# Unread matmuls of zeros in seven other forms ahead of an attention and two-MLP kernel

## The chip, the cores and the metric

The kernel runs on one core of a Trainium2 chip. The metric is the device time of one launch in microseconds (us). A core has five engines that run side by side, each through an instruction list of its own, in order: TensorE (PE in the profile, its weight loads PEld), VectorE (DVE), ScalarE (ACT), GpSimd (POOL) and SyncE (SP), which here only issues DMAs. An engine waits for another by semaphores, which the tile framework sets from what each instruction reads and writes. TensorE's clock has two levels, 2.4 and 1.2 GHz; the profile gives the granted level as a share of the upper one (1.00 and 0.50).

## The reference, cut to what matters

Three parts, one after the other, in float32:

```python
# q, k, v [4, 8, 576, 64], f [4, 8, 576]
scores = q @ k.T / 8 + cum_i - cum_j        # cum = cumsum(log(clip(f))), causal
x = softmax(scores) @ v                     # -> [2304, 512]
h = x @ w_in                                # [512, 2048]
g = where(h >= 1, h, where(h <= -1, 0, (h + 1) ** 2 / 4))
x = g @ w_out                               # [2048, 512]
# the top two of 8 experts per token, softmax of their noisy logits as weights
out[t] += weight * (max(x[t] @ w1[e], 0) @ w2[e])   # w1 [512, 1024], w2 [1024, 512]
```

## The kernel before, in words

Most products are made with each operand split into a high and a low part of type float32r, three products for one. Attention works through 16 pairs of heads. For a pair, q and k come in by DMA, TensorE transposes them (`turn`, L377, and `turn_tail`, L381), ACT writes the high parts (`split_hi`, L397), DVE the low ones (`split_lo`, L401), a DMA swaps halves of k (`k2`, L421), POOL makes the differences of the cumulated decay (`diff`, L439, from `crow` and `ccol`, with a mask at L444), TensorE makes the scores (L468, L469; L457 for the last tile), DVE adds and takes the minimum (L482), ACT takes the exponential (L491), TensorE transposes it (L501), ACT and DVE split it into `aX` and `aY` (L524, L528), and TensorE multiplies with the values (L547). The cumulated sums themselves come from DVE's clip (L290), ACT's logarithm (L292) and DVE's scan (L293); for the first pair TensorE spreads the rows (L343) and turns them into columns (L300), which DVE copies into `ccol` (L304). The first MLP's units (L682, L708) and the conversion of its weights (L644 to L652) are mixed in between; routing and the experts come after.

The order of every engine's list up to the experts is worked out when the kernel is built: `job` registers a piece of work for an engine with its inputs, outputs and an estimated cost, `in_order` plays a model of the engines and returns the jobs in one order, and `emit` writes them out. Engines then keep to their lists. Ahead of the jobs only a few constants are made (L74 to L84), among them `ident`, the identity.

In `emit`, ahead of a job of TensorE that the model says comes after a gap, products `ident` x `ident` are written into the bank `idle` (L217); nobody reads them. The first of these stand ahead of the transposes of the first k. Each such float32 product appears in the trace as two instructions.

`zeros` (L313) is a set of POOL jobs: memsets of `qt`, `vnat`, `e4`, then `aX[0]`, `aX[1]`, `aY[0]`, `aY[1]`. In POOL's list small memsets and iotas (L357, L739 to L747) follow, and then the first `diff`.

PSUM's banks are rings: `psS` (tag "s", two banks, scores), `psT` (two, transposes), `psA` ("av", one), `psH` ("h", one, which `idle` holds at first) and `psY` (two; the first pairs' transposes of q and k are in it).

Of the kernel before, what the change touches and what calls it, by code (L numbers as in the profile page):

```python
# [8 lines left out]
F32 = mybir.dt.float32  # L9
# [7 lines left out]
BIG = 1.0e9  # L17
# [5 lines left out]
def kernel(  # L23
# [56 lines left out]
    # rows 2 r and 2 r + 1 of a product, summed  # L80
# [14 lines left out]
    class Ring:  # L95
        """Buffers that take turns."""
# [8 lines left out]
    class Buf:  # L105
        """One use of a ring's buffer; the tile is there when the first job that names it is emitted."""
# [8 lines left out]
    class Job:  # L115
        """Instructions of one engine that are emitted together."""
# [7 lines left out]
    def job(eng, cost, at, fn, r=(), w=(), size=0):  # L124
        """r, w: what the job reads and writes: buffers, (buffer, part), or names."""
        j = Job(len(jobs), eng, cost, fn, at, size)
        jobs.append(j)
        for x in r:
            if x in writer:
                j.deps.add(writer[x])  # L130
            readers.setdefault(x, []).append(j)
        for x in w:
            if x in writer:
                j.deps.add(writer[x])
            j.deps.update(readers.get(x, ()))
            writer[x], readers[x] = j, []
        j.deps.discard(j)
        for x in (*r, *w):
            b = x[0] if isinstance(x, tuple) else x
            if isinstance(b, Buf) and b not in j.bufs:  # L140
                if not b.jobs:
                    j.new.append(b)
                b.jobs.append(j)
                b.left += 1
                j.bufs.append(b)
        return j

    def in_order():
        """The jobs in the order in which engines that take whatever is due first would start them."""
# [7 lines left out]
        for j in jobs:  # L157
            # a bank isn't taken before all that its users wait for is on its way
            held = {d for b in j.new if b.held for u in b.jobs for d in u.deps if d.no < j.no}
            for d in (held | {b.jobs[0] for b in j.bufs}) - j.deps - {j}:  # L160
                d.after.append(j)
                j.left += 1
# [4 lines left out]
        while len(out) < len(jobs):  # L167
            best = None
            for e, todo in ready.items():
                pick = None  # L170
                for j in todo:
                    t = max(j.ready, free[e])
                    for i, b in enumerate(j.new):
                        # buffers of the same ring come one after the other
                        k = len(b.ring.tenants) + sum(o.ring is b.ring for o in j.new[:i])
                        if b.ring.fixed and b.no != k:
                            t = 1e9
                        k -= b.ring.bufs
                        if k >= 0:
                            o = b.ring.tenants[k]  # L180
                            t = max(t, o.free) if not o.left else 1e9
                    if t < 1e9 and (pick is None or (t, j.at, j.no) < pick[:3]):
                        pick = t, j.at, j.no, j
                if pick and (best is None or pick[:3] < best[:3]):
                    best = pick
# [20 lines left out]

    def emit():
        # TensorE's clock halves after a stretch of little work: until the first MLP takes the bank,
        # products that nobody reads keep each stretch busy enough
        idle, last, busy = psH.tile([P, 512], F32, name="idle", tag="h"), WARM2, []  # L210
        for j in in_order():
# [61 lines left out]
    # Y: head 0's last TAIL queries, the queries before them of the head at hand, head 1's last TAIL queries  # L273
    aY = [ap1.tile([P, NKB, YQ // TAIL + 1, TAIL], F32R, name=f"aY{i}") for i in range(2)]
    e4 = ap1.tile([P, NKB * P], F32, name="e4")
    # the last query tile holds both heads' last TAIL rows; each head's stationary operand is zero in the other's columns
# [45 lines left out]
    class Pair:  # L322
        """Two heads; their queries go through in tiles of P rows, the last tile holds the last TAIL rows of both."""
# [7 lines left out]
        def add(self):  # L331
# [7 lines left out]
            for j in range(2 * (self.n == 0)):  # L339
                # the first rows by way of the tensor engine  # L340
# [24 lines left out]
        def prep(self):  # L365
            """Transposed q' = -q / 8 and k in (hi, lo) parts.

            t = q'.k + cum_j - cum_i has the row's maximum as its minimum, negated."""
# [14 lines left out]
            # head 0: [hi; lo], head 1: [lo; hi] on the partitions  # L383
# [19 lines left out]
            for i, w in enumerate((1, 0, 2)):  # L403
# [7 lines left out]
                for j in range(2):  # L411
                    # parts of qk: queries, keys, the last keys
# [12 lines left out]
        def tile(self, n, j, it):  # L425
            """Decay differences and scores; softmax's exponentials; transposed, in (hi, lo) parts."""
# [5 lines left out]
            # cum_j - cum_i, with BIG where j is behind i  # L432
# [100 lines left out]
        def values(self, n, j, x):  # L533
            """Attention times values, transposed: the sum of the two halves of the partitions."""
# [3 lines left out]
            for kb in range(nkb):  # L538
                # the first column that isn't all zero; head 0's last queries come first
# [22 lines left out]
        def finish(self):  # L562
            """1 / (sum + 1e-9), by head and tile, as rows; the second head's last rows are its last tile's first."""
# [32 lines left out]
    class Quarter:  # L596
        """QF hidden units' weights in a slot."""
# [29 lines left out]
    def convert_quarter(q, at, pace):  # L627
        """A quarter's float64 weights, given as int64 bits, as exact pairs of float32r; also kept in DRAM.

        The high word as a float32, times 2**-112, has float64's exponent less 896 in its bits:  # L630
        float32's, with the fields three bits too low. Magnitudes under 2**-119 come out tiny."""
# [23 lines left out]
    def load_x(at, c, x, eng):  # L655
        """A chunk of the attention's output, transposed, in (hi, lo) parts."""
# [9 lines left out]
    class Unit:  # L666
        """Two blocks of hidden units of one chunk: up, the nonlinearity, down into the chunk's sums."""
# [4 lines left out]
        def up(self, at, j):  # L672
# [16 lines left out]
            # max(h, 1) * ((clip(h, -1, 1) + 1) / 2) ** 2  # L689
# [34 lines left out]
    def routing_consts():  # L724
        for i, src in enumerate((moe2_w_gate, moe2_w_noise)):
            dma(30, lambda i=i, src=src: nc.sync.dma_start(wg[:, :, i * E:(i + 1) * E], src.rearrange("(c p) e -> p c e", p=P)), [("xd", 0, 0)], [("wg", i)], size=16384 * 8)
        # no key of the last block is visible to the queries before the last tile
# [32 lines left out]
    class Route:  # L760
        """Top two experts of some tiles of tokens, their weights and places in the experts' lists."""
# [7 lines left out]
        def turn(self, at, t, xt, dep):  # L769
            """One tile's rows, transposed, and its logits."""  # L770
# [20 lines left out]
        def chain(self, at):  # L791
# [20 lines left out]
            # log1p(exp(z)) = log(u) * e / (u - 1), u = 1 + e; e where u = 1  # L812
# [31 lines left out]
            # the largest two, the first of equals first  # L844
# [18 lines left out]
            # places in the experts' lists: the tile's rows before, and the tile's totals  # L863
# [23 lines left out]
            # the place r goes to partition r % P, unit r / P  # L887
            @part("DVE", 0.36 * K, ["ecol"], ["base"])
            def _():
# [4 lines left out]
                if self.seal:  # L894
                    # the first two experts' first EARLY places are for the tokens up to here; what stays empty is a pad
                    ts(base[:, 0, :2], base[:, 0, :2], float(EARLY), None, op0=OP.max)
# [102 lines left out]
    def stream(at, rate, units, end=True):  # L999
        """Pieces of units; a unit's down after the next one's up, in the next call's if this isn't the end."""  # L1000
# [53 lines left out]
    def expert_jobs(e, rings, stages, at, pace, deps=()):  # L1054
        """An expert's w1 [DM, F2] and w2 [F2, DM] as (hi, lo) with the contraction on partitions."""
# [69 lines left out]
    def counts():  # L1125
        """How many blocks each expert has."""
# [6 lines left out]
        # the second expert's second block of CH is always done  # L1133
        nc.vector.scalar_tensor_tensor(odd[:, 1:2], units[:, 1:2], 4.0, odd[:, 1:2], op0=OP.is_gt, op1=OP.mult)
        # 2: the odd block has P / 2 rows at most
# [11 lines left out]
    def early_block(at, e, r):  # L1147
        """The first EARLY places of one of the first two experts, while the rest is on its way."""
# [98 lines left out]
    # work by step; within a step by key  # L1247
# [16 lines left out]
    def bank_tr():  # L1264
        """A bank for transposes."""
# [3 lines left out]
    def expert(e, pool, lands):  # L1269
        """w1 [DM, F2] and w2 [F2, DM] as (hi, lo) with the contraction on partitions, and the work in pieces."""  # L1270
# [28 lines left out]
    def fetch(n, dst, g, cols, wait):  # L1299
        """Rows of the list's tokens, transposed, in (hi, lo) parts."""  # L1300
# [16 lines left out]
    def when(n, i, cols):  # L1317
        """The first of two tiles of rows is through before the last piece of work."""
# [17 lines left out]
    def blend(n, cols, ys):  # L1336
        """Rows of the result as they are, plus the weighted rows of an expert."""
# [6 lines left out]
    def combine(n, py, cols, quick=False):  # L1344
        """Rows of the result plus an expert's weighted rows."""
# [16 lines left out]
    def body256(x, W, cols, side=None, quick=False):  # L1362
# [19 lines left out]
        def down(fp, k):  # L1382
            hh, hl = (h.rearrange("p (j t) -> p j t", j=2) for h in hs[fp % 2])
            # of the last two blocks of hidden units, one tile of rows after the other
# [65 lines left out]
    def body64(x, W, idc, g):  # L1450
        """P / 2 rows: (hi, lo) side by side, so that the products with the weights' hi part take one pass."""
# [48 lines left out]
    def last_units():  # L1500
        """The last unit's column of each list."""
# [33 lines left out]
    for e in range(E):  # L1535
        nblk, nodd = size[2 * e:2 * e + 2]

        # the block that is always done here
# [77 lines left out]
```

## Time and profile before

| | |
|---|---|
| Median of 3 runs | 1269.96 us (1266.02 to 1273.33) |
| Span of the profiled execution, first to last instruction | 1250.6 us |
| The median less that span | 19.4 us |
| PE busy | 1166.6 us, 93% |
| DVE, POOL, ACT busy | 65%, 47%, 41% |
| Mean granted clock of TensorE | 0.981 |

The profile was taken of one execution; the time of that execution as a launch is not listed beside the three, so the median stands for it: what lies around the span is then 19.4 us. A row of the timeline is: start us, duration us, engine, line, operation, output and inputs, count, and in brackets how long the engine was idle before and who released it; neighbouring instructions of one line are merged into one row. A matmul's duration contains its way through the array; how often one can follow the other is read from the distance of starts.

### The profile page before, as it was taken

Reading aid. Unit: us, or ns where it says so; the run is one execution under the profiler, and the core shown is the slowest. Engines: PE = TensorE matmul, PEld = TensorE weight load, DVE = VectorE, ACT = ScalarE, POOL = GpSimd, SP = SyncE. Lnnn points to the kernel's source line nnn. Section 1 sums busy time; section 2 is a strip of 40 time slices with the busy share of each in tenths; the row PEclk is TensorE's granted clock in tenths of the full one; section 3 lists DMA queues with packets and bytes.
Section 4 is the critical chain, followed back from the end, with each engine's and each line's share of the span. In section 5 each row is a group of like instructions: output and inputs, shape, how many; then the busy total and the mean of one; then the engine's idle time right before and its main releaser. Section 6 shows DMA issues by size and latency. Waiting matters only on the chain. (4 is left out here: it accounts for less than half of the span.)

```text
span 1250.6 us, 21814 instructions
## 1 busy us (share of the span) xinstructions
PE 1166.6 (93%) x7527; PEld 1040.7 (83%) x7527; DVE 813.6 (65%) x1814; ACT 517.5 (41%) x1151; POOL 587.8 (47%) x724
## 2 busy tenths in 40 slices
PE   8787799999999999999999999999999999899994
PEld 6676688889888988998999998888888888788893
DVE  7989889986876657734565685373555555774432
ACT  6767776667654664623344351120312121330000
POOL 7779777767474654620300114353434343434221
PEclk8989999999999999999999999999999999999997
DMA  6777798855745434664022143262434343642121
GB/s 169 205 221 202 235 312 247 272 167 153 219 158 150 119 111 134 191 259 162 16 78 67 43 128 122 71 212 91 158 113 155 119 163 107 218 156 70 54 73 38
DMA packets 135314, 185.56 MB, mean 148 GB/s; under 512 B 72063, under 2 KB 81569, under 8 KB 135157
## 3 DMA queue, kind: packets, MB, share of 16 engines
q1 hardware_dynamic: 122692, 148.85, 38.3%
q0 software_dynamic: 12464, 34.76, 8.5%
q8 instruction: 81, 1.33, 0.4%
q14 instruction: 77, 0.62, 0.2%
HBM read 134.76 MB, written 41.65 MB: 141 GB/s over the span
## 5 line engine op out<-in xcount | busy, mean ns | idle before, releaser
L682 PEld LDWEIGHTS h<-xc,w 128*128 128x128 f32 x1344 | 170.8, 191 | 10.2 <-issue 5.4
L682 PE MATMUL h<-xc,w 128*128 128x256 f32 x1344 | 173.6, 285 | 4.2 <-DVE ga L696 4.1
L439 POOL TENSOR_TENSOR D<-crow,ccol 128x128 f32<-128x128 f32 (+4 forms) x160 | 136.4, 859 | 60.5 <-DVE mn L482 51.8
L708 PE MATMUL y<-w,gh 128*128 128x512 f32 x480 | 156.6, 407 | 0.0
L1379 DVE TENSOR_SCALAR hs<-eh 128x512 fp32r<-128x512 f32 x64 | 44.0, 688 | 131.9 <-PE eh L1375 131.9
L921 POOL DMA_INDIRECT lists<-ent,ai x36 | 36.7, 1019 | 147.4 <-DVE ai L912 122.3
L1262 POOL TENSOR_TENSOR ys<-ys,prev 128x512 f32<-128x512 f32 x32 | 41.8, 1306 | 132.6 <-ACT ys L1324 123.0
L708 PEld LDWEIGHTS y<-w,gh 128*128 128x128 f32 x480 | 84.9, 191 | 14.5
L708 PE MATMUL y<-w,gl 128*128 128x512 f32 x240 | 95.5, 398 | 0.0
L699 POOL TENSOR_TENSOR gl<-ga,gh 128x512 fp32r<-128x512 f32 x48 | 62.5, 1302 | 66.3 <-ACT gh L697 61.1
L695 ACT ACTIVATE ga<-ga,half 128x512 f32<-128x512 f32 x72 | 52.1, 723 | 97.7 <-DVE ga L694 78.5
L1262 ACT CAST e<-w 128x512 fp32r<-128x512 f32 x96 | 56.2, 620 | 76.9 <-DMA w<-in_moe_w_dram 72.5
L1375 PE MATMUL eh<-xF,e 128*128 128x256 f32 x672 | 84.8, 282 | 3.1 <-PEq L1581 3.1
L1389 PE MATMUL y<-e,hs 128*128 128x512 f32 x336 | 85.5, 400 | 1.0 <-DVE hs L1379 1.0
L694 DVE TENSOR_SCALAR ga<-h 128x512 f32<-128x512 f32 x60 | 41.4, 689 | 69.0 <-PE h L682 63.5
L1375 PEld LDWEIGHTS eh<-xF,e 128*128 128x128 f32 x672 | 82.2, 189 | 4.7 <-issue 3.5
L491 ACT ACTIVATE et<-et,mn 128x128 f32<-128x128 f32 (+3 forms) x128 | 72.0, 564 | 16.7 <-DVE mn L482 15.7
L482 DVE CUSTOM_DVE_ANT_0 et<-s,D 128x128 f32<-128x128 f32 (+3 forms) x128 | 61.2, 484 | 23.9 <-PE tr L501 12.3
L1262 DVE TENSOR_TENSOR e<-w,e 128x512 fp32r<-128x512 f32 x96 | 72.8, 795 | 5.7 <-ACT e L1262 5.7
L1389 PEld LDWEIGHTS y<-e,hs 128*128 128x128 f32 x336 | 60.5, 188 | 13.9 <-issue 1.4
L1332 POOL DMA_INDIRECT out_dram<-ys,ids x32 | 33.7, 1053 | 77.2 <-DVE ys L1262 38.4
L1144 POOL DMA_INDIRECT xg<-x2d,ids x48 | 50.5, 1052 | 29.4 <-issue 22.3
(307 smaller groups left out, 2794.6 us busy)
## 6 DMA issues: line engine op xcount, KB each, us to landing
w<-in_moe_w_dram SPq DMA_DIRECT2D x128, 256.0 KB
w<-wsd SPq DMA_DIRECT2D x24, 1024.0 KB
wsd<-w SPq DMA_DIRECT2D x16, 1024.0 KB
crow<-cumd SPq DMA_DIRECT2D x30, 288.0 KB
k<-qk SPq DMA_DIRECT2D x60, 144.0 KB
st<-in_moe_w_in_dram SPq DMA_DIRECT2D x16, 512.0 KB
st<-in_moe_w_out_dram SPq DMA_DIRECT2D x16, 512.0 KB
D<-rsd SPq DMA_DIRECT2D x32, 144.0 KB
```

The lines of the kernel that those rows point to most:

```text
L439: nc.gpsimd.tensor_tensor(Dt.t[r, :w], self.crow[i].t[r, :w], ccol[r, it, h:h + 1].to_broadcast([r.stop - r.start, w]), op=OP.subtract)
L482: nc.vector.tensor_tensor_reduce(out=ev()[:, c0:c0 + pw], in0=ps.t[:, :pw], in1=Dt.t[:, c0:c0 + pw], scale=1.0, scalar=HUGE, op0=OP.add, o ...
L491: nc.scalar.activation(ev()[:, :w], ev()[:, :w], AF.Exp, bias=mn.t[:, 0:1], scale=-1.0, accum_out=self.sm.t[:, j, it:it + 1])
L682: nc.tensor.matmul(h.t[:, j, :], self.quarter.up(2 * self.fp + j, db, wi), x[:, xi, db, :], start=(i == 0), stop=(i == 3 * NB - 1))
L695: job("ACT", 0.62, at - 2.4, lambda: nc.scalar.activation(a.t, a.t, AF.Square, bias=half, scale=0.5), w=[a])
L699: lambda: e.tensor_tensor(gl.t, a.t, r32(gh.t), op=OP.subtract), [a, gh], [gl])
L708: nc.tensor.matmul(self.py[t].t, g[:, j, ts], self.quarter.down(f, wi), start=(self.first and j == 0 and i == 0), stop=(self.last and j == ...
L1144: nc.gpsimd.indirect_dma_start(out=xg[gi], out_offset=None, in_=x2d[:rows, :], in_offset=bass.IndirectOffsetOnAxis(ap=idc, axis=0), **skip)
L1262: fn(*args)
L1375: nc.tensor.matmul(p[:, j, :], wt[:, db, fs], x[:, xi, db, :], start=(i == 0), stop=(i == 3 * NB - 1))
L1379: nc.vector.tensor_scalar(hh, ph[fp % 2], 0.0, None, op0=OP.max)
L1389: nc.tensor.matmul(py[t], h[:, j, ts], wt[:, fb, :], start=(fb == 0 and i == 0), stop=(fb == NF - 1 and i == 2))
```

## The change

Ahead of the first job, `emit` calls a new function `probes`. It takes the bank that `idle` holds, one use of `psA`'s bank and one of `psS`'s, has VectorE fill `aX[0]` with zeros, and issues 65 matmuls of these zeros and 4 transposes of `ident` on TensorE. Nobody reads what they write. With the float32r tile as operands (`z`) there are 16 of 512 columns, 5 each of 128, 256 and 512, 8 of 512 columns over half the rows (upper and lower half in turn), and 4 of 512 that alternate with the transposes. With the same bytes as float32 (`zf`) there are 3 of 256 columns, 3 over the upper half of the rows, 8 over upper and lower half in turn, and 8 that fill the left and right half of the output's partitions in turn. All else in the diff is comments and docstrings.

```diff
+    def probes(bank):
+        b2 = psA.tile([P, 512], F32, name="probe2", tag="av")
+        b3 = psS.tile([P, 512], F32, name="probe3", tag="s")
+        z = aX[0].rearrange("p i c -> p (i c)")
+        zf = r32(z)
+        nc.vector.memset(zf, 0.0)
+        mm = nc.tensor.matmul
+        for _ in range(16):
+            mm(bank, z[:, :P], z, start=True, stop=True)
+        for n in (128, 256, 512):
+            for _ in range(5):
+                mm(b2[:, :n], z[:, :P], z[:, :n], start=True, stop=True)
+        for _ in range(3):
+            mm(bank[:, :256], zf[:, :P], zf[:, :256], start=True, stop=True)
+        for _ in range(3):
+            mm(b2[:, :256], zf[:64, :P], zf[:64, :256], start=True, stop=True)
+        for _ in range(4):
+            mm(bank[:, :256], zf[:64, :P], zf[:64, :256], start=True, stop=True)
+            mm(b3[:, :256], zf[64:, :P], zf[64:, :256], start=True, stop=True)
+        for _ in range(4):
+            mm(b2[:64, :256], zf[:, :64], zf[:, :256], start=True, stop=True)
+            mm(b2[64:, :256], zf[:, 64:P], zf[:, :256], start=True, stop=True)
+        for _ in range(4):
+            mm(bank, z[:64, :P], z[:64], start=True, stop=True)
+            mm(b3, z[64:, :P], z[64:], start=True, stop=True)
+        for _ in range(4):
+            mm(b2, z[:, :P], z, start=True, stop=True)
+            nc.tensor.transpose(bank[:, :P], ident, ident)
+
     def emit():
         idle, last, busy = psH.tile([P, 512], F32, name="idle", tag="h"), WARM2, []
+        probes(idle)
         for j in in_order():
```

## Rows read from the trace of the kernel before

**Rows 1.** Timeline of TensorE (PE) from the start to the first scores.

```profile
1.47 4.16 PE L217 MATMUL idle<-ident 128*128 128x128 f32 x22 [1.47 <-DVE ident L76]
5.47 0.60 PE L377 MATMUL y<-ident,kn 128*128 128x128 f32 x4
...
8.92 1.12 PE L343 MATMUL s<-xf,ident 32*128 32x512 f32 x2 [2.51 <-DVE xf L293]
9.88 0.37 PE L300 MATMUL tr<-ident,xf 32*128 32x32 f32 x4
...
13.42 1.22 PE L217 MATMUL idle<-ident 128*128 128x128 f32 x4
14.30 0.56 PE L468 MATMUL s<-qk 128*128 128x256 f32 x1
...
18.24 0.61 PE L217 MATMUL idle<-ident 128*128 128x128 f32 x4
```

**Rows 2.** Timeline of VectorE (DVE), the same stretch.

```profile
1.77 0.06 DVE L84 MEMSET half<- 128x1 f32 x1
...
1.89 0.54 DVE L291 MEMSET k<- 32x576 f32 x1
...
8.90 0.68 DVE L401 SCALAR_TENSOR_TENSOR qk<-y,qk 64x512 fp32r<-64x512 f32 x1
...
11.36 0.32 DVE L304 COPY ccol<-tr 128x160 f32<-128x160 f32 x1
...
17.14 0.56 DVE L482 CUSTOM_DVE_ANT_0 et<-s,D 128x384 f32<-128x384 f32 x1 [1.06 <-PE s L469]
...
18.21 0.69 DVE L482 CUSTOM_DVE_ANT_0 et<-s,D 128x512 f32<-128x512 f32 x1 [0.50 <-PE tr L501]
```

**Rows 3.** Timeline of GpSimd (POOL) and ScalarE (ACT), the same stretch.

```profile
1.77 0.99 POOL L313 MEMSET aX<- 128x512 f32 x2
...
6.50 0.34 POOL L747 IOTA e<- 128x8 int32 x1
...
7.39 1.19 ACT L397 ACTIVATE qk<-y 64x512 fp32r<-64x512 f32 x2
...
11.84 0.97 POOL L439 TENSOR_TENSOR D<-crow,ccol 128x128 f32<-128x128 f32 x2 [5.00 <-DVE ccol L304]
```

**Rows 4.** Stretches: bounds, length, each engine's busy us (count), granted clock, DMA share, GB/s.

```profile
9.90:11.90 2.00, 1.91 (x13) 1.34 (x12) 1.88 (x8) 1.82 (x4) 0.06 (x1) 0.86 0.47 107
...
14.20:17.20 3.00, 3.00 (x14) 2.92 (x13) 0.79 (x5) 2.11 (x5) 2.84 (x5) 0.50 0.52 117
17.20:18.30 1.10, 1.10 (x6) 0.88 (x5) 0.60 (x3) 0.15 (x1) 1.02 (x2) 0.55 0.78 157
...
93.00:125.00 32.00, 24.09 (x165) 19.98 (x163) 30.13 (x83) 25.26 (x71) 28.88 (x41) 1.00 0.71 199
```

**Rows 5.** TensorE's timeline at 700 us, products of 512 columns.

```profile
699.71 0.40 PE L708 MATMUL y<-w,gh 128*128 128x512 f32 x1
699.95 0.40 PE L708 MATMUL y<-w,gl 128*128 128x512 f32 x1
700.18 2.97 PE L682 MATMUL av<-xc,w 128*128 128x256 f32 x24
```

**Rows 6.** The chain that ended last, one piece: start, us, what.

```profile
1162.82 5.62 PE eh L1375 x48
```

**Rows 7.** Line L217: count, shortest/median/longest ns, first and last start.

```profile
L217 PE MATMUL idle<-ident x186: 271/275/582, 1.5 to 135.5; 128*128 128x128 f32 x186
```

**Rows 8.** Waits, first 300 us (us in total, times, longest): SyncE's queue.

```profile
SPq L644 <- POOL w L652: 35.1, 14, 7.0
...
SPq L317 <- PE av L381: 13.5, 5, 7.0
SPq L317 <- PE y L381: 6.6, 3, 3.3
```

**Rows 9.** Waits of TensorE, first 300 us.

```profile
PE s L468 <- DVE mn L482: 8.7, 9, 3.2
```

## The prediction

> **What bounds the kernel now.** I read TensorE's timeline from the start first, because the change stands ahead of everything else in that list. It has three things to see [rows 1]: the unread products from 1.47 us, the transposes of the first k at 5.47, and the first scores at 14.30. Then the same stretch on the engines that feed the scores. DVE begins the low parts of k at 8.90 and copies `ccol` at 11.36 [rows 2]; POOL has been through its memsets and iotas by 6.84 (6.50 + 0.34), sits idle for 5.00 us until `ccol` is there, and starts the first difference at 11.84 [rows 3]. So the head is one chain through all engines: k's transposes, ACT's and DVE's splits, `ccol`, POOL's differences, DVE's minimum. Last I read who waits for whom in the first 300 us. SP, which issues all loads, waits 35.1 us for POOL to be through with the buffers of converted weights, and 13.5 and 6.6 us for TensorE's transposes to free the buffers of k and q [rows 8]; TensorE waits longest for DVE's minimum, 8.7 us [rows 9]. In a stretch of 32 us there TensorE is busy for 24.09 and DVE for 30.13 [rows 4]. No queue in this stage runs free of the engines: what starts late stays late.
>
> **What is added on TensorE.** Unread products do run: 186 of them stand in the trace of before [rows 7]. I price the new ones by distance between starts.
> - float32r, 512 columns: three starts lie 0.47 us apart over two [rows 5], 0.235 each. There are 16 + 5 + 4 = 25 over the whole height: 5.88 us. The 8 over half the rows would be 1.88 at the same distance.
> - float32r, 256 columns: 48 in 5.62 us [rows 6], 0.117 each; five are 0.59. At 128 columns no float32r product is in the trace. Half of 0.117 and the 0.235 of 512 columns are the ends (0.29 and 1.18 for five); I take 0.117, the nearest row, 0.59.
> - float32, 256 columns: not in the trace either. `idle`'s are float32 with 128 columns, two instructions per product. Four of them at 18.24 us took 0.61 to the end of the last [rows 1]; less its own 0.27 [rows 7] that is 0.34 over three starts, 0.113. Twice the columns and two instructions make 0.45 a product. L343 checks it from the other side: 512 columns, two instructions, from 8.92 to 9.88 [rows 1], so 0.48 for half. There are 3 + 3 + 8 + 8 = 22: 9.9 us.
> - Four transposes: four of k's took 0.60 to the end of the last [rows 1], less 0.27 and over three starts 0.11 each: 0.44.
>
> Together 5.88 + 1.88 + 0.59 + 0.59 + 9.9 + 0.44 = 19.3 us if each waits for the one before. To this comes a slow beginning. The first 22 `idle` instructions took 4.00 us (1.47 to 5.47) where 22 x 0.113 would be 2.5 [rows 1]. The other group of four, at 13.42, needed 0.88 to the next start, 0.22 each [rows 1], in a stretch around the granted clock 0.50, which is 1.2 GHz [rows 4]. So the list begins at the lower level, and what I pay for that is the 1.5 us that the 22 paid. 20.8 us.
>
> The unsettled price is that of the halves. No pair of half-height or half-width products on different halves is in the trace. L343, with 32 rows, is no faster for its small height: 0.48 per instruction of 512 columns, as the check above says. By this nearest row each of the 24 products (8 float32 by rows, 8 by columns, 8 float32r by rows) costs what a whole one does, 3.6 + 3.6 + 1.88 us, which is in the sum. The other end is that the two of a pair run at once: half of that, 4.54 us less. I take the row, and keep the other as a rival. The Trainium skill ("TensorE: Matmul & The Clock Gate", Part 3: Packing small matmuls) says that products in different row groups or column groups of the array overlap; its "TensorEngine Tiling (Array Packing)" (Key Properties) says that a change of the tiling mode drains the engine. By the first the sum is 16.3 us, and by the second each of five changes adds about 0.16 (0.27 less 0.11), 0.8 us by estimate; no row here shows either.
>
> **Where it lies.** The zeros come first: `half` ends on DVE at 1.83, and 32 x 576 zeros took 0.54 [rows 2], so 512 columns about 0.48. The probes begin near 2.4 and end at 23.2. The 22 `idle` instructions stand behind them, now at the upper level: 2.5 us. k's transposes start at 25.7 instead of 5.47, 20.2 late.
>
> Not all of that goes on, since what used to come late is waiting by then. DVE's first low part follows after 0.6 of transposes, half of ACT's 1.19 [rows 3] and 0.1, at 27.0; before it was at 8.90, held back by the scan. It is 18.1 late. POOL has a wait of its own: its memset of `aX[0]` overwrites what the probes read, so the whole list behind it stands until 23.2. From 1.77 to 6.84 POOL needed 5.07 us [rows 3], so it is free at 28.3. `ccol` ended 2.78 after DVE's first low part (11.68 less 8.90 [rows 2]), so now at 29.8, behind that: POOL's memsets hide, with 1.5 us to spare, and the first difference at 29.9 is 18.1 late as well. If the probes ended without freeing `aX[0]`, POOL would cost up to that much more. The loads behind POOL, ACT and TensorE on SP shift alike [rows 8]. VectorE's extra memset costs nothing: DVE waits for f and later for TensorE anyway.
>
> A part comes back. From about 11.3 to 18.2 us the granted clock was 0.50 (worked out from the 0.86, 0.50 and 0.55 of three stretches [rows 4]), not long after TensorE had stood idle for 2.51 us [rows 1]. DVE waited 1.06 and 0.50 for TensorE in it [rows 2]. After 23 us of work and with all inputs at hand the clock should be full there: 1.56 back (none, if it falls again). 18.1 - 1.6 = 16.5 us. Nothing later changes: the lists are the same.
>
> The profiled span, 1250.6, becomes 1267.1. With the 19.4 us by which the median lies above that span, 1286.5; I say 1286.
>
> **The rivals.**
> - The pairs run at once. 4.5 us less on TensorE, which leaves 12.0: 1282. For it: the two of a pair write different banks or partitions. Against: only L343's price, which is of single products.
> - The clock falls during the probes. In the trace it fell to 0.50 soon after the 32-row products of L343, behind an idle stretch, and came back only near 18.2, though TensorE was busy for 3.00 of 3.00 us [rows 4]. If products of half the height don't hold it either, a stretch like that one (6.9 us at the lower level) costs 3.4 us, and the 1.6 at the first scores doesn't come back: 1286.5 + 5.0 = 1291.5.
> - The delay is taken back, and the kernel isn't slower. One mechanism: TensorE's gaps in the first 150 us (about 8 us in 32 [rows 4]) would have to be gaps before loads that SP issues when it likes; two such stretches would swallow the 16 us, and 1270 would stay. It decides from the point where SP's weight loads are issued as early as before. Against: these gaps end with DVE, and SP waits for POOL and TensorE [rows 8, 9]. To be faster, it would also need fewer stretches at 0.50 later on, and one such stretch is worth 3.4 us.
> - The change doesn't do what it says: the probes are dropped, and 1270 stays. The 186 unread products that ran speak against it.
>
> **How the numbers follow.** Forecast 0.47, pairs at once 0.32, clock 0.14, taken back 0.05, dropped 0.02. Each case has some 3.5 us to either side from the spread of the runs before (1266.02 to 1273.33). The low end is the pairs' 1282 less 3.5 and a little, 1278; the high end the clock's 1291.5 with 1.5 us of dearer 128-column and float32 products, 1293. The forecast's own range is 1282 to 1290. About 0.5%, 6.35 us, can be told from no change: slower means over 1276.3. The three cases that are slower hold 0.93, the other two mostly fall within, 0.05, and 0.02 stays for faster.
>
> **What would show it.** In the changed trace: the first probe near 2.4 us; starts 0.235 apart at 512 columns; the half-height and half-width stretches at 3.6, 3.6 and 1.9 us, or at half of these; k's transposes near 25.7; POOL's memset of `aX` just before; the first difference near 30; the first scores' stretch at clock 1.00; from there every landmark the same 16 us late to the last instruction. The prediction is wrong if the delay at 30 us and that at 280 us differ by more than 4 us, or if the probes take under 16 or over 24 us.

## The result: slower, by less than forecast, and the profile after

The changed kernel takes 1279.27 us (median of 10 runs, 1271.66 to 1283.84) against 1266.9 for the kernel before (10 runs, 1262.59 to 1273.33). The ratio is 1.0086 [1.0062, 1.011]: 10.9 us more, 7.9 to 13.9. It was timed a second time later (e10 below): 1.0115 [1.0082, 1.0148], 14.6 us. The forecast was 16. Of the 6.7 us between the 1286 named and the 1279.27 measured, 3.1 are the median of before, which came out lower with more runs; the other 3.7 are the forecast's own (12.4 us between the medians against 16; by the ratio it is 5 too many).

TensorE's timeline from the start, in the changed kernel; "..." stands for rows of the same forms:

```profile
2.43 5.26 PE L216 MATMUL idle<-aX 128*128 128x512 f32 x16 [2.43 <-DVE aX L213]
7.53 2.47 PE L219 MATMUL probe<-aX 128*128 128x128 f32 x15
9.84 1.46 PE L221 MATMUL idle<-aX 128*128 128x256 f32 x6
11.22 1.34 PE L223 MATMUL probe<-aX 64*128 64x256 f32 x5
12.20 0.48 PE L226 MATMUL probe<-aX 64*128 64x256 f32 x1
12.40 0.38 PE L223 MATMUL probe<-aX 64*128 64x256 f32 x1
12.52 0.38 PE L226 MATMUL probe<-aX 64*128 64x256 f32 x1
12.62 0.38 PE L225 MATMUL idle<-aX 64*128 64x256 f32 x1
12.73 0.38 PE L226 MATMUL probe<-aX 64*128 64x256 f32 x1
...
14.44 0.43 PE L228 MATMUL probe<-aX 128*64 128x256 f32 x1
...
14.92 0.38 PE L228 MATMUL probe<-aX 128*64 128x256 f32 x1
14.93 0.38 PE L229 MATMUL probe<-aX 128*64 128x256 f32 x1
...
16.01 0.38 PE L229 MATMUL probe<-aX 128*64 128x256 f32 x1
16.32 0.49 PE L231 MATMUL idle<-aX 64*128 64x512 f32 x1
...
17.44 0.50 PE L234 MATMUL probe<-aX 128*128 128x512 f32 x1
...
18.92 2.62 PE L248 MATMUL idle<-ident 128*128 128x128 f32 x22
21.37 0.60 PE L408 MATMUL y<-ident,kn 128*128 128x128 f32 x4
...
28.61 0.56 PE L499 MATMUL s<-qk 128*128 128x256 f32 x1
```

The probes take from 2.43 to 18.92, 16.5 us and not 20.8. The whole-height forms cost what was worked out: 5.10 us to the next form for the first 16, 2.31 for the mixed 15 (1.18 + 0.59 + 0.59 forecast), 1.38 for the three float32 ones. The halves did not: their price was set too high. At 14.92 and 14.93 a left and a right half start together; the upper and lower halves of the float32 rows start 0.11 apart where one alone needs 0.21. From the first pair (12.20, 14.44, 16.32) to the next form the three stretches are 2.24, 1.88 and 1.12 us against 3.6, 3.6 and 1.88.

GpSimd (POOL) and VectorE (DVE) in the same stretch, which answer to [rows 2, 3]:

```profile
19.03 0.99 POOL L344 MEMSET aX<- 128x512 f32 x2 [17.19 <-PE probe L234]
23.25 0.68 DVE L432 SCALAR_TENSOR_TENSOR qk<-y,qk 64x512 fp32r<-64x512 f32 x1 [17.87 <-ACT qk L428]
26.19 0.97 POOL L470 TENSOR_TENSOR D<-crow,ccol 128x128 f32<-128x128 f32 x2 [2.29 <-DVE ccol L335]
...
31.45 0.56 DVE L513 CUSTOM_DVE_ANT_0 et<-s,D 128x384 f32<-128x384 f32 x1 [1.06 <-PE s L500]
32.52 0.69 DVE L513 CUSTOM_DVE_ANT_0 et<-s,D 128x512 f32<-128x512 f32 x1 [0.50 <-PE tr L532]
```

k's transposes are 15.9 us late, DVE's first low part 14.35, the first difference 14.35, the first scores 14.3. GpSimd is held by the probes for 17.19 us and then still waits 2.29 for `ccol`. The waits of 1.06 and 0.50 that I let go are there as before. Some stretches (bounds, length, busy us of PE, PEld, DVE, ACT, POOL with counts, granted clock, DMA share, GB/s; one row left out) show why:

```profile
21.40:22.20 0.80, 0.80 (x9) 0.56 (x7) 0.00 (x0) 0.19 (x1) 0.80 (x2) 1.00 0.00 0
...
23.50:25.50 2.00, 0.99 (x8) 0.78 (x7) 1.88 (x7) 1.72 (x6) 0.40 (x4) 1.00 0.60 150
25.50:27.70 2.20, 2.20 (x6) 1.02 (x4) 1.53 (x8) 1.49 (x4) 1.51 (x5) 0.56 0.43 96
27.70:30.00 2.30, 2.30 (x11) 2.27 (x11) 0.94 (x4) 1.93 (x4) 2.23 (x5) 0.50 0.56 128
```

TensorE comes out of the probes at 1.00, is busy for 0.99 of 2.00 us around the 32-row products, and by the first scores it is at 0.50, 1.2 GHz, as it was without probes [rows 4].

The profile's span is 1282.0 us, 31.4 more than before's. That is no measure of the change: the 1282.0 belong to a run of 1283.84 us, so only 1.8 us lie around a span, and the execution profiled before, 1250.6, was shorter than any of the 10 timed beside it (the shortest, 1262.59, would have a span near 1260.8). What differs is the second half. First and last starts of the experts' first block, in this order, with the span: before 1250.6, changed 1282.0, and of the experiments below e6 (no probes) 1264.1, e9 (probes four times) 1314.0, e2 1269.8 and e11 1279.7 (one and the same program):

```profile
L1193 PE MATMUL h<-xF,w x96: 274/281/365, 723.2 to 760.9; 128*128 128x256 f32 x96
```
```profile
L1224 PE MATMUL h<-xF,w x96: 274/281/365, 739.9 to 778.7; 128*128 128x256 f32 x96
```
```profile
L1202 PE MATMUL h<-xF,w x96: 274/281/365, 723.4 to 761.5; 128*128 128x256 f32 x96
```
```profile
L1225 PE MATMUL h<-xF,w x96: 274/281/365, 780.8 to 818.5; 128*128 128x256 f32 x96
```
```profile
L1224 PE MATMUL h<-xF,w x96: 274/281/365, 741.8 to 779.6; 128*128 128x256 f32 x96
```
```profile
L1224 PE MATMUL h<-xF,w x96: 274/281/365, 740.8 to 778.6; 128*128 128x256 f32 x96
```

From the last of these starts to the end before took 489.7 us, the changed kernel 503.3, but e6 without a single probe 502.6 and e9 495.5; e2 and e11, the same program, took 490.2 and 501.1. These up to 13 us come and go from one execution to the next, probes or not; the two profiles can be compared up to here and no further.

### The profile page after: what moved, and what is told of

It is laid out like the page before. It is cut to its first block, busy times and chain, and to the rows that moved or that the text cites. A ratio compares the mean times of both kernels' runs of the same rounds, so it can differ in the third digit from the quotient of the medians.

```text
span 1282.0 us, 21998 instructions
## 1 busy us (share of the span) xinstructions
PE 1194.5 (93%) x7618; PEld 1059.9 (83%) x7618; DVE 812.4 (63%) x1815; ACT 517.4 (40%) x1151; POOL 586.7 (46%) x724
## 5 line engine op out<-in xcount | busy, mean ns | idle before, releaser
L713 PEld LDWEIGHTS h<-xc,w 128*128 128x128 f32 x1344 | 172.1, 193 | 10.8 <-issue 5.9
L739 PEld LDWEIGHTS y<-w,gh 128*128 128x128 f32 x480 | 85.3, 192 | 14.7 <-ACT ya L1021 0.2
L522 ACT ACTIVATE et<-et,mn 128x128 f32<-128x128 f32 (+3 forms) x128 | 72.0, 564 | 15.9 <-DVE mn L513 14.3
L513 DVE CUSTOM_DVE_ANT_0 et<-s,D 128x128 f32<-128x128 f32 (+3 forms) x128 | 61.1, 485 | 21.0 <-PE tr L532 12.5
L1175 POOL DMA_INDIRECT xg<-x2d,ids x48 | 49.2, 1025 | 29.8 <-issue 23.7
```

The costliest lines, as they stand in the source:

```text
L513: nc.vector.tensor_tensor_reduce(out=ev()[:, c0:c0 + pw], in0=ps.t[:, :pw], in1=Dt.t[:, c0:c0 + pw], scale=1.0, scalar=HUGE, op0=OP.add, o ...
L522: nc.scalar.activation(ev()[:, :w], ev()[:, :w], AF.Exp, bias=mn.t[:, 0:1], scale=-1.0, accum_out=self.sm.t[:, j, it:it + 1])
L713: nc.tensor.matmul(h.t[:, j, :], self.quarter.up(2 * self.fp + j, db, wi), x[:, xi, db, :], start=(i == 0), stop=(i == 3 * NB - 1))
L739: nc.tensor.matmul(self.py[t].t, g[:, j, ts], self.quarter.down(f, wi), start=(self.first and j == 0 and i == 0), stop=(self.last and j == ...
L1175: nc.gpsimd.indirect_dma_start(out=xg[gi], out_offset=None, in_=x2d[:rows, :], in_offset=bass.IndirectOffsetOnAxis(ap=idc, axis=0), **skip)
```

## Experiments

All edits are to the changed kernel unless said otherwise. "Head" is the first difference on GpSimd less 11.84 us [rows 3]; "end" the ratio's excess times the median of before measured in the same hour on the same chip. The expectations weigh three theories: A, what the head loses, the end loses one for one; B, about a quarter of it comes back before the end; C, a fixed 2 to 3 us comes back, or (its first reading) the head of the kernel before is usually that much later than in its one profile.

| run | head | end, 95% interval |
|---|---|---|
| changed | +14.4 | +10.9 [7.9, 13.9] |
| e1, no pairs | +10.5 | +9.7 [6.3, 13.1] |
| e2, pairs on one side | +20.0 | +13.9 [9.2, 18.5] |
| e3, twice | +30.0 | +27.8 [23.7, 32.1] |
| e4, fillers behind the probes | +15.2 | +14.7 [8.6, 20.8] |
| e5, first 31 | +6.6 | +11.8 [7.5, 16.1] |
| e6, zeros only | +0.7 | +2.2 [-1.0, 5.3] |
| e7, before with fillers | +1.1 | +2.8 [-0.4, 6.0] |
| e8, other tile | +15.0 | +13.3 [9.1, 17.5] |
| e9, four times | +60.1 | +57.0 [53.2, 60.8] |
| e10, changed again | +15.3 | +14.6 [10.4, 18.7] |
| e11, pairs on one side again | +20.2 | +15.2 [10.8, 19.5] |

**Do the halves run at once?** e2 puts both products of a pair on the same half:

```diff
-            mm(b3[:, :256], zf[64:, :P], zf[64:, :256], start=True, stop=True)
+            mm(b3[:, :256], zf[:64, :P], zf[:64, :256], start=True, stop=True)
...
-            mm(b2[64:, :256], zf[:, 64:P], zf[:, :256], start=True, stop=True)
+            mm(b2[:64, :256], zf[:, 64:P], zf[:, :256], start=True, stop=True)
...
-            mm(b3, z[64:, :P], z[64:], start=True, stop=True)
+            mm(b3, z[:64, :P], z[:64], start=True, stop=True)
```

> Both products of each pair use the same half of the array (upper rows, left columns), so that the two can't lie side by side. If a pair was cheap because its two products ran at once, the three stretches go from 1.9, 1.9 and 1.1 us to about 3.7, 3.7 and 1.9, the probes end 4.4 us later (near 23.3 us), and the end is 18.7 us later than without probes by theory A, 14.2 by theory B. If half a product simply costs half, the stretches and the 14.3 us at the head stay as they are.

TensorE's timeline of e2, where "..." again stands for the same forms:

```profile
13.93 0.59 PE L225 MATMUL idle<-aX 64*128 64x256 f32 x2
14.37 0.59 PE L226 MATMUL probe<-aX 64*128 64x256 f32 x2
...
17.48 0.65 PE L228 MATMUL probe<-aX 128*64 128x256 f32 x2
...
21.07 0.49 PE L231 MATMUL idle<-aX 64*128 64x512 f32 x1
21.41 0.39 PE L232 MATMUL probe<-aX 64*128 64x512 f32 x1
21.64 0.39 PE L231 MATMUL idle<-aX 64*128 64x512 f32 x1
...
23.11 0.51 PE L234 MATMUL probe<-aX 128*128 128x512 f32 x1
...
27.05 0.60 PE L408 MATMUL y<-ident,kn 128*128 128x128 f32 x4
```

A float32 half product alone costs 0.43 us, a float32r one 0.23, as much as whole ones, and the three stretches are 3.55, 3.59 and 2.04 us: together 9.2, close to the 9.1 in the prediction's sum. So it is not the size but the other half's being free that made the pairs cheap; nor is it a bank, for the two of a row pair still write different banks here. k's transposes come 5.7 us later than in the changed kernel; 1.3 of it is the start (the first row of L225 at 13.93 instead of 12.62, since the first probes ran longer at the lower level), and the other 4.4 are the pairs. At the end the timed difference to the changed kernel was small, which called for a repetition, next to the changed kernel on one chip:

> The probes with both products of a pair on the same half once more: 20.0 us later at the first difference, timed 13.9 before. Theory A: 20 us later, and more than the changed kernel by 5.7; B: 15, more by 4.3. If 13.9 comes again, beside a changed kernel at 11, something takes back what the serial pairs cost.

> The changed kernel once more, beside the others. First difference near 26.2 us, 14.4 later than without. Theory A: 14.4 us later at the end; B: 10.8; C: 11.8. Which chip and which hour also moves the difference by a few us, so this says how far one timing of it can be trusted.

The changed kernel came out at 14.6 [10.4, 18.7], the one-sided at 15.2 [10.8, 19.5]. The first agrees with its head of 15.3; the second is 5 below its 20.2, as e2 was 6 below its 20.0. At the experts' first block the two traces are still 18.7 and 17.7 us behind before (779.6 and 778.6 against 760.9): 1.3 and 2.5 less than their heads, within the scatter of single traces, and not 5 or 6.

e1 leaves the pairs out:

```diff
-        for _ in range(4):
-            mm(bank[:, :256], zf[:64, :P], zf[:64, :256], start=True, stop=True)
-            mm(b3[:, :256], zf[64:, :P], zf[64:, :256], start=True, stop=True)
...
-            mm(bank, z[:64, :P], z[:64], start=True, stop=True)
-            mm(b3, z[64:, :P], z[64:], start=True, stop=True)
```

> The 24 products on half the rows or columns that came in turn are left out of the probes. In the changed kernel they took from 12.20 to 17.44 us. Theory A (what the head loses, the end loses, one for one): the first difference on GpSimd comes at 21.0 us instead of 26.2 and the kernel ends 9.1 us later than the one without probes. Theory B (about a quarter is taken back before the end, as the timed 10.9 us against 14.3 at the head suggests): 6.9 us later. On the clock: if the probes' half products are what lets the clock fall before the first scores, it stays at 1.00 there now; if the 32-row products and the gap behind k's transposes do it, it falls to 0.50 as before.

The first difference came at 22.31 (1.3 us above the expectation, the slower start again), the end 9.7 [6.3, 13.1] later: nearer to A's 9.1, but with B's 6.9 inside. The clock fell without the half products too:

```profile
20.00:22.00 2.00, 1.36 (x7) 1.07 (x7) 1.85 (x8) 1.50 (x4) 0.02 (x1) 0.71 0.52 127
22.00:24.00 2.00, 2.00 (x3) 0.83 (x3) 0.94 (x5) 1.18 (x2) 1.69 (x5) 0.50 0.40 90
```

**Does the delay reach the end?** e3 issues the list twice, e9 four times, e5 only its first 31, e6 only the memset.

```diff
+        for _ in range(2):          # e9: range(4)
             for _ in range(16):
                 mm(bank, z[:, :P], z, start=True, stop=True)
...
```

> The whole list of probes is issued twice. The second pass runs at the upper clock throughout, about 15 us, so the first difference comes near 41 us, 29 us later than without probes. Theory A: the end is 29 us later. Theory B: 22 us later, a quarter taken back. If something fixed absorbs a few us once (theory B2), 26 us.

> The whole list of probes four times. A pass at the upper clock took 15.05 us in the run with two, so the first difference comes near 71.9 us, 60.1 later than without probes. Theory A (one for one): the end is 60 us later, 56 to 64 with the scatter seen so far. Theory B (a quarter comes back): 45 us. Theory C (a fixed 2 to 3 us comes back): 57 us.

e3: 27.8 [23.7, 32.1]. e9: 57.0 [53.2, 60.8], and its first difference came at 71.91, where expected. That a quarter comes back (22 and 45) is out. That a fixed 2 to 3 us does (26 and 57) fits as well as one for one.

The traces can be read for it ahead of the part that scatters, at attention's last exponential (`et`, the last start; before, changed, e9):

```profile
L491 ACT ACTIVATE et<-et,mn x128: 385/564/745, 15.6 to 525.1; 128x128 f32<-128x128 f32 x32, 128x256 f32<-128x256 f32 x32, 128x384 f32<-128x384 f32 x32, 128x512 f32<-128x512 f32 x32
```
```profile
L522 ACT ACTIVATE et<-et,mn x128: 389/562/738, 29.9 to 539.9; 128x128 f32<-128x128 f32 x32, 128x256 f32<-128x256 f32 x32, 128x384 f32<-128x384 f32 x32, 128x512 f32<-128x512 f32 x32
```
```profile
L523 ACT ACTIVATE et<-et,mn x128: 384/564/739, 75.7 to 582.4; 128x128 f32<-128x128 f32 x32, 128x256 f32<-128x256 f32 x32, 128x384 f32<-128x384 f32 x32, 128x512 f32<-128x512 f32 x32
```

The changed kernel is 14.8 us behind there (head 14.4), e9 57.3 (60.1), e3 31.6 (30.0), e2 20.2 (20.0), e11 17.3 (20.2), e10 16.9 (15.3), e8 13.2 (15.0), e1 8.1 (10.5), e5 7.5 (6.6) and e6 0.1 ahead (0.7 behind). Some 500 us later each of these delays is the head's, to 3 us on either side, and the quarter of B is out here too. (e4 has 12.5 for 15.2 and e7 4.6 for 1.1; their fillers go on behind the head.)

```diff
         for n in (128, 256, 512):
             for _ in range(5):
                 mm(b2[:, :n], z[:, :P], z[:, :n], start=True, stop=True)
-        for _ in range(3):
...
```

> Only the first 31 probes (float32r, whole height) stay. They end near 10.4 us, k's transposes come near 12.7 and the first difference near 17.5 us, 5.7 later than in the profile without probes. Theory A (one for one): the end is 5.7 us later. Theory C (the timed differences so far lie 0.5 to 6.1 us under the head's delays, on average 2.6, because the head of the kernel without probes is usually later than in its one profile, or because a fixed 2.6 us comes back): 3.1 us later. Theory B (a quarter comes back): 4.3.

> The memset of zeros on VectorE stays, all probes go. No theory expects a change: within 2 us of the kernel without probes, first k transposes near 5.4 us. Its profile is a second look at the head without probes: by theory C's first reading the first difference comes some 2 to 3 us after 11.84; by the others at 11.8.

e5 ended 11.8 [7.5, 16.1] later behind a head of 6.6 (its first difference came at 18.48, 1 us above the expectation): more than the head lost, the opposite of anything coming back; in its trace the 7.5 us at attention's end are near the head, so that trace has no such excess ahead of the experts. e6, in the same hour, was 2.2 [-1.0, 5.3] above before. Its head lay 0.7 us behind the profile of before: GpSimd's first memset of `aX` waits 0.59 us for VectorE's zeros. So, as far as two profiles tell, that profile's head is a usual one and the first reading of C falls.

**Does GpSimd's wait count?** e8 reads another tile, whose memset stands last:

```diff
-        z = aX[0].rearrange("p i c -> p (i c)")
+        z = aY[1].rearrange("p k i r -> p (k i r)")[:, :512]
```

> All probes, but they read aY[1] instead of aX[0]: GpSimd's memset of aY[1] is the last of the four, so GpSimd has done 2.7 of its 5.1 us of memsets and iotas before it is held. In the changed kernel it then still waits 2.29 us for ccol, so the hold is hidden: the first difference stays near 26.2 us and the end 11 to 14 us later than without probes, as in the changed kernel. If the hold did cost something, both come up to 2.7 us earlier.

GpSimd's timeline of e8:

```profile
2.71 1.69 POOL L344 MEMSET aY<- 128x1920 f32 x1
19.63 1.70 POOL L344 MEMSET aY<- 128x1920 f32 x1 [15.23 <-PE probe L234]
26.79 0.97 POOL L470 TENSOR_TENSOR D<-crow,ccol 128x128 f32<-128x128 f32 x2 [4.87 <-DVE ccol L335]
```

What it has done earlier it waits longer for `ccol`: 4.87 instead of 2.29. The first difference is 0.6 later (the probes' start once more), the end 13.3 [9.1, 17.5]. The hold is hidden, as forecast.

The traces of this kind also show where the catch-up between k's transposes and the first difference comes from. VectorE's clip of f, the first step towards `ccol`, in the kernel before, the changed one and e8:

```profile
2.67 4.10 DVE L290 TENSOR_SCALAR k<-D 32x576 f32<-32x576 f32 x1 [0.25 <-DMA D<-in_f_dram]
```
```profile
2.90 0.38 DVE L321 TENSOR_SCALAR k<-D 32x576 f32<-32x576 f32 x1
```
```profile
2.90 1.81 DVE L321 TENSOR_SCALAR k<-D 32x576 f32<-32x576 f32 x1
```

It ends 0.31 us after GpSimd's last memset of that stretch in before (6.77 and 6.46), in e6 (7.43 and 7.12) and in e8 (4.71 and 4.40); where the probes hold all these memsets back, it takes 0.38 us. In the kernel before, ACT's logarithm, then k's high parts and VectorE's scan wait for it, and the first low part starts 3.43 us after k's transposes instead of 1.88. What the two engines share there no run shows, and none moves the memsets behind the clip without probes.

**The clock at the first scores.** e4 adds fillers behind the probes, e7 to the kernel before:

```diff
+                nth += 1
+                if 2 <= nth <= 8:
+                    for _ in range(2):           # e7: 8 ahead of the 3rd job
+                        nc.tensor.matmul(idle[:, :P], ident, ident, start=True, stop=True)
```

> Two more unread full-height products ahead of each of TensorE's 2nd to 8th job, 14 in all, 3.2 us at the upper clock, some of it in gaps where TensorE waits. If the clock falls before the first scores because TensorE does little work there (32-row products and waits), it stays at 1.00 through them, VectorE no longer waits 1.5 us for scores, and the end comes 0 to 1 us earlier than with the probes alone. If it falls all the same, the fillers cost 1 to 2 us.

> The kernel without probes, with 20 more unread full-height products: 8 ahead of TensorE's 3rd job (in the gap where it waits for the scan, 6.4 to 8.9 us), two ahead of each other one from the 2nd to the 8th. If little work there is what drops the clock, it stays at 1.00 through the first scores (14 to 18 us), and with the 2.7 us that came back behind the head where fillers were added to the probes, the end is 1 to 2.5 us earlier than without. If it falls all the same, the end is 0 to 2 us later.

In both the clock stays up. The stretch with the first scores, e4, then e7:

```profile
30.00:32.00 2.00, 2.00 (x16) 1.81 (x16) 1.11 (x3) 1.57 (x3) 0.79 (x3) 1.00 0.35 78
```
```profile
16.00:18.00 2.00, 2.00 (x15) 1.81 (x16) 1.13 (x2) 1.54 (x3) 0.68 (x3) 1.00 0.62 141
```

In sum nothing is won by it. e7's timeline has the first scores at 17.39 instead of 14.30 [rows 1], because the fillers stand between the jobs of a chain:

```profile
8.24 2.05 PE L226 MATMUL idle<-ident 128*128 128x128 f32 x16
...
17.39 0.36 PE L473 MATMUL s<-qk 128*128 128x256 f32 x1
```

The full clock itself does give something. First scores and VectorE's fourth minimum, in e4 and (the minimum) in e7:

```profile
31.28 0.36 PE L504 MATMUL s<-qk 128*128 128x256 f32 x1
33.62 0.69 DVE L518 CUSTOM_DVE_ANT_0 et<-s,D 128x512 f32<-128x512 f32 x1
```
```profile
19.73 0.69 DVE L487 CUSTOM_DVE_ANT_0 et<-s,D 128x512 f32<-128x512 f32 x1
```

The scores are 2.67 us later than in the changed kernel (28.61), the minimum only 1.10 (32.52); in e7 it is 3.09 and 1.52 against the kernel before (18.21 [rows 2]). Between the two marks 1.57 us come back in both.

e7 timed 2.8 us above before [-0.4, 6.0], e4 14.7 [8.6, 20.8], no better than the probes alone. My expectation for both was wrong: the lower level is worth 1.6 us there, less than the 3 us of fillers that lift it. No run here beats the kernel before.

## Why the prediction was right or wrong

- **That it slows the kernel, and in which way: right.** The order of events is the forecast one: probes, 22 fillers at the upper level (2.45 us, forecast 2.5), k's transposes, first difference on `ccol` and not on GpSimd's memsets.
- **The prices of whole products: right.** 0.43 us for a float32 product of 256 columns (0.45 forecast); the mixed 15 of float32r within 0.05 us of the forecast, the last four products and four transposes within 0.1; to the first 16 the lower level at the start (starts 0.43 us apart up to 5.16, 0.23 after) added 1.34 us to 3.76 (1.5 forecast). That start varied by up to 1.5 us from run to run (L219 from 7.53 in the changed kernel, 8.98 in e11).
- **"By this nearest row each of the 24 products costs what a whole one does": this step failed.** It holds for two products on one half (e2: 0.43 and 0.23, 9.2 us in all), not for two on different halves. The term was 9.1 us and measured 5.24, 3.9 less. I had only a row of a product alone, took it for the price of a pair, and set the other end at half: the Trainium skill's rule ("TensorE: Matmul & The Clock Gate", Part 3: Packing small matmuls) was the right one here. By it the sum was 16.3, or 17.1 with the changes of tiling mode ("TensorEngine Tiling (Array Packing)", Key Properties); the trace has 16.5. This rival had 0.32 and the forecast 0.47; it should have been the other way round.
- **"1.56 back" at the first scores: wrong.** The step that failed here is that the clock would be full after 23 us of work: it was 1.00 through all half products (11.2 to 17.4 us), so the clock rival's reason did not come true either, but it fell again behind the probes, in the head's own stretch of 32-row products and waits, with the half products or without (e1). Which of the two lets it fall no run separates. The size was right, 1.57 in e4 and e7 where fillers kept the clock up; the fillers cost more than that.
- **The catch-up of 2.1 us between k's transposes and the first difference: right in kind,** 1.55 measured (15.9 less 14.35, and 3.43 less 1.88). Before, the low part did wait for the scan; behind that stood the clip's 4.10 us beside GpSimd's memsets. That VectorE's extra memset costs nothing holds with the probes; without them (e6) the clip ends and the first difference starts 0.66 us later.
- **One for one to the end: nearly right.** Forecast less the 3.9 of the pairs and plus the clock is 16.5 - 3.9 + 1.56 = 14.2; the head measured 14.35, the times 10.9 and 14.6, e8 13.3. The sign named for it held: the delay was 14.35 us at the first difference and 14.1 at GpSimd's last piece of the first MLP's weights (last start of L652 at 269.3 us before, 283.4 in the changed kernel). Over all runs a fixed part of 0 to 3 us may come back. At the experts' first block the lag of the changed kernel was 17.8 and of e9 57.6 (heads 14.4 and 60.1): scatter of a few us to both sides arises before that. That every landmark stays as late down to the last instruction can't be read from single traces.
- **"The 19.4 us by which the median lies above that span": a wrong reading that cancelled.** A launch is 1.8 us longer than its span; the profiled execution had been a short one.

What stays open: why the one-sided pairs cost 14 to 15 us at the end behind a head of 20 in both timings, and e5 11.8 behind one of 6.6, while twice and four times the list pass on 93 and 95%; and what makes the experts' half 490 us in some executions and 503 in others.

## What to carry to other kernels

Work at the head of one engine's list, ahead of the first step of a chain through all engines, costs its duration less what was waiting for other reasons: find what the first common step waits for, and price to there. A row of an operation alone is no price for two that use different halves of a unit; when no row shows a pair, give the half price at least equal weight. Look also at what the delayed engines no longer disturb: here memsets that came later left VectorE's clip at 0.38 us instead of 4.10. And take a profile's span for one execution out of many: compare landmarks ahead of the part that scatters, and times from runs taken together.

## What was not expected of the hardware

Left and right halves of TensorE's columns start within 0.01 us of each other (14.92 and 14.93), and 16 float32 half-width instructions take 1.88 us to the next form. Upper and lower halves of the rows overlap too, though the two instructions of one float32 product do not: starts 0.11 us apart, each instruction with its own half at 0.21. By the trace the first instruction on the lower rows (L226, 12.20) even starts ahead of two on the upper rows that stand before it in the list, the last of L223 (12.40) and the first of L225; the traces of e3, e9 and e10 show the same order. Between stretches of different tiling 0.1 us more than the distance of starts passes (16.01 to 16.32 against 0.21). And a clock that was full after 16 us of dense work was at 0.50 some 4 us after k's transposes began, with TensorE idle for 1.01 of the last 2.00 us shown before it fell (23.50 to 25.50).
